# Attention and two expert layers on one core: filler matmuls in batch 0, 12 transposes a unit, and a later place for w_out's scale

## The chip, the cores and the metric
The kernel runs on one core of one Trainium2 chip. The metric is the device time of one execution in microseconds. The core's engines are TensorE (PE), VectorE (DVE), ScalarE (ACT), GpSimd (POOL) and SyncE (SP, which here issues the DMAs); each works through a queue of its own in order, and waits on semaphores where it needs another engine's result.

## What is computed
The reference in short; the three parts are chained.

```python
# q, k, v: (4 batches, 8 heads, 576, 64)
out_d  = softmax(q_d k_d^T / 8) v_d          # q_d, k_d, v_d: means over 4 neighbours, 144 rows
local  = softmax(where(|i - j| < 4, q k^T / 8, -1e9)) v
x      = (repeat(out_d, 4) + local)           # -> 2304 tokens x 512

xn     = x / sqrt(mean(x * x) + 1e-6) * rms_g
g      = xn @ w_gate                          # 512 x 1536
x      = (g * sigmoid(g) * (xn @ w_val)) @ w_out   # 1536 x 512

h      = relu(x @ w_in)                       # 512 x 2048
out    = (s * h * h + b) @ w_out2             # 2048 x 512
```

## The kernel before
**Precision.** The products of the two expert layers run in 16-bit floats: each operand is split into a high and a low part, and three of the four partial products are summed, so one product of 128 x 288 over 512 takes 12 matmuls (`pg` for the gate, `pvl` for the value, L708). The weights come as 8-byte numbers; `fetch` (L614) loads a chunk and turns it into f32 on ACT (L624, L625) and DVE (L626, L630), and `halves` (L125) scales it and splits it into the two parts, either on ACT and DVE (L127, L128) or on POOL and ACT (L130 to L132).

**Stages.** Attention of batch 0 comes first, in four units of two heads (`early_unit`). A unit loads q, k and v, turns q and k by PE (`tp`, copied by ACT at L428), forms the local scores `sl` and the downsampled scores `sd`, two softmaxes, turns the probabilities (`tpl`, `tpd`), and multiplies with v (`pvd`, `pl`). When four units are through, `norm` sums the squares (`ssn`, L570), takes the root on POOL (r, then three bf16 parts rp, L575 to L581), spreads it by PE (`rb`, L586) and writes the scaled tokens into X (L595). Then the blocks of 288 tokens follow. Blocks 0 and 1 go together (`main01`): 24 pairs of gate and value products, for the four parts of the weights in turn (three pairs for each part and block), and then the out product (`po`, L729) of both blocks, 144 matmuls each. Attention of batch 1 is emitted in small steps between them.

**Weights.** The generator `rest` (L804) emits the preparation of the four weight parts (`prep_gv`: 8 chunks of 384 KB, the maximum by PE as `st`, then the splits), and then of w_out (`weigh`: 12 chunks of 512 KB, each squared by ACT into accw; `abo` casts the sums on POOL, `so` adds them on PE at L671, DVE makes the scale sgo, and 12 splits follow). The steps of `rest` are pulled one by one from the loops that emit attention and pairs; two at every step of `main01`.

**What sets the order.** The program is written as a list of tiles and instructions; when it is built, a scheduler puts each engine's instructions into one fixed order, by the order in which the code emits them, by priorities, and by its estimate of when inputs are ready. `queued(name)` (L312) holds back all that is emitted in it until two instructions noted in `gates[name]` are issued. Part 0 of the weights is under no gate; part 1 is under gates[1], the second softmax of batch 0's last unit; parts 2 and 3 and w_out are under gates[2], the first half of the norm (L597). On the chip nothing changes places any more: an instruction that waits holds all that is behind it on its engine.

**Buffers.** PSUM tiles named tp, tpl and tpd of batch 0, st, so, pg, pvl and po share one pool of four; sl has two, pl and pvd one together, sd, ssn and rb one together. The SBUF tile u, which a pair needs from ACT's tanh to POOL's low part, has three. Chunks whose 8-byte form does not fit in place are staged in a ring of four and two more (`staging`, L606).

Of the kernel before, what the change touches and what calls it, by code (L numbers as in the profile page):

```python
# [20 lines left out]
NP = H // 2  # L21
# [20 lines left out]
EARLY = 2  # L42
CAP0 = 100
# [26 lines left out]
def kernel(  # L70
# [49 lines left out]
    ENG = [(dve, pool)] * NPART + [dve]  # L120
# [110 lines left out]
    def load_unit(b, hp, qkf, vd, vw):  # L231
        h0 = 2 * hp
        for t, src in enumerate((q, k)):
            for h in range(2):
                if b == 0:
                    sp.dma_start(out=qkf[:, t, h], in_=src[b, h0 + h].rearrange("(p c) d -> p c d", c=6))
                else:
                    sp.dma_start(out=qkf[:, t, :, h, :], in_=src[b, h0 + h].rearrange("(c p) d -> p c d", p=GR))
# [105 lines left out]
    def values_d(vdh, PdT, scale, pairs=LL):  # L344
        pvd = pV.tile([128, SD], F32, tag="v", name="pvd")
        n_ = 2 * len(pairs) - 1
# [13 lines left out]
    def values_l(b, hp, js, vh, PlT, od, scale, pairs=LL):  # L360
        pl = pV.tile([128, 320], F32, tag="v", name="pl")
        for j in js:
# [26 lines left out]

    def turned(b, n, name):  # L390
        if b == 0:
            return mmp.tile([128, 3, n], F32, tag="mm", name=name)
        return pS.tile([128, 3, n], F32, tag="s", name=name)

    def early_unit(b, hp, sq_sum):
# [18 lines left out]
        for t in range(2):  # L414
            qT = qkT[:, S * t:S * t + S]
            qT = qT.rearrange("p (a c) -> p c a", c=6) if b == 0 else qT.rearrange("p (c a) -> p c a", c=6)
# [20 lines left out]
        def local(js):  # L437
            sl = pS.tile([128, 5, WIN], F32, tag="s", name="sl")
            for p0 in (0, 64):
# [18 lines left out]
        sd = pX.tile([128, 3, SD], F32, tag="x", name="sd")  # L458
        for o, q0 in ((0, 0), (1, 64), (2, SD - 64)):
# [22 lines left out]
        if b == 0 and hp == NP - 1:  # L482
            gates[1] = tuple(last)
        yield
        od = values_d(vs.unsqueeze(1), PdT, 0.25, ((0, 0),))
# [562 lines left out]
```

## Time and profile before
| what | value |
|---|---|
| median of 3 runs | 1107.35 us (1106.99 to 1108.79) |
| the profiled execution's own time | 1106.15 us |
| its span, first to last instruction | 1104.4 us |
| PE busy | 1003.6 us (91%) |
| DVE busy | 592.8 us (54%) |
| ACT busy | 521.4 us (47%) |
| POOL busy | 339.5 us (31%) |
| mean granted TensorE clock | 0.926 |

The times of runs hold what lies around the span, 1.75 us in the profiled execution. Busy time is an average over the whole run; the stages differ, so the windows of the trace are read stage by stage. The granted clock is the share of full speed (2.4 GHz) that TensorE was given; 0.50 is 1.2 GHz. Names are those of the program; W is the tile W1, which holds the weights' chunks and, early on, other things of the same place. Block 2's first matmul starts at 301.6 us, and blocks 2 to 7 and the second expert layer make up the rest.

### The profile page before, as it was taken

The numbers are of one execution on the slowest core, as the hardware profiler recorded it, in microseconds if no ns is written. First come the engines' busy times: TensorE is split into PE (matmuls) and PEld (weight loads), VectorE is DVE, ScalarE is ACT, GpSimd is POOL, SyncE is SP. The second block draws the span as 40 slices with busy tenths as digits, with TensorE's granted clock in tenths as the row PEclk, the third lists the DMA queues.
The fourth block names the chain that finished last, engine by engine and source line by source line (L and its number), as shares of the span: only waits on it lengthen the run. The fifth ranks groups of instructions, "written<-read, shape, count | busy, mean of one in ns | idle before, by whom it ended". The sixth has DMA issues, their size and how long they took to land.

```text
span 1104.4 us, 20466 instructions
## 1 busy us (share of the span) xinstructions
PE 1003.6 (91%) x8204; PEld 685.4 (62%) x8206; DVE 592.8 (54%) x1255; ACT 521.4 (47%) x1174; POOL 339.5 (31%) x433
## 2 busy tenths in 40 slices
PE   5775686899988989898999999999999999999998
PEld 4663564678866767676778667755554545455553
DVE  3766996642187764576762876656341414234241
ACT  3655778643255554355644777756140413223140
POOL 6435674246144545453644213621000000000000
PEclk7675885899988989998999999999999999999999
DMA  8733456100035542145511442400000000000000
GB/s 195 212 87 98 137 156 174 36 20 13 1 67 91 116 88 49 39 84 90 117 38 39 134 134 77 160 32 1 29 1 29 1 20 11 10 20 1 29 1 29
DMA packets 120431, 73.59 MB, mean 67 GB/s; under 512 B 102161, under 2 KB 108305, under 8 KB 120337
## 3 DMA queue, kind: packets, MB, share of 16 engines
q1 hardware_dynamic: 120336, 72.29, 26.1%
q8 instruction: 64, 1.05, 0.4%
q14 instruction: 31, 0.25, 0.1%
HBM read 54.97 MB, written 4.72 MB: 54 GB/s over the span
## 4 chain that ended last, share of the span: by engine, by line
PE 66%; DMA 13%; DVE 10%; ACT 6%; issue 3%; POOL 2%; SPq 1%; DVEq 0%; POOLq 0%; ACTq 0%
PE y L1010 17%; PE ph L990 16%; PE po L729 8%; PE pvl L708 8%; PE pg L708 8%; DMA stg<-in_moe_w_in_dram 3%; DMA qkT<-qk 3%; DMA stg<-in_moe_w_out_dram 2%; DVE W L630 2%; DVE stg L626 2%; DMA vd<-in_v_dram 2%; ACT stg L625 1%; PE pl L367 1%; PE pvd L352 1%; ACT W L624 1%
## 5 line engine op out<-in xcount | busy, mean ns | idle before, releaser
L708 PEld LDWEIGHTS <-W 128*128 128x128 f16 x2304 | 229.1, 101 | 88.9 <-issue 23.9
L990 PE MATMUL ph<-X,W 128*128 128x384 f16 x1152 | 196.6, 326 | 0.4 <-DVE s4o L673 0.3
L708 PE MATMUL pg<-X,W 128*128 128x288 f16 x1152 | 170.2, 296 | 15.0 <-DVE u L715 11.0
L708 PE MATMUL pvl<-X,W 128*128 128x288 f16 x1152 | 172.3, 295 | 0.6 <-DVE m L647 0.5
L990 PEld LDWEIGHTS <-W 128*128 128x128 f16 x1152 | 112.6, 98 | 81.5 <-issue 1.2
L1010 PE MATMUL y<-W 128*128 128x512 f16 x648 | 151.6, 379 | 0.0
L729 PEld LDWEIGHTS <-W 128*128 128x128 f16 x1152 | 111.5, 98 | 31.1 <-issue 2.8
L729 PE MATMUL po<-g,W 128*128 128x288 f16 x1008 | 129.0, 287 | 1.6 <-DVE u L715 0.9
L994 ACT ACTIVATE r<-ph 128x384 f32<-128x384 f32 x96 | 47.0, 490 | 175.8 <-PE ph L990 126.1
L719 POOL TENSOR_TENSOR g<-u,g 128x288 f16<-128x288 f32 x84 | 72.1, 859 | 140.3 <-ACT g L718 106.1
L1010 PEld LDWEIGHTS <-W 128*128 128x128 f16 x648 | 63.4, 98 | 70.9
L190 DVE SCALAR_TENSOR_TENSOR r<-ph,r 128x384 f32<-128x384 f32 x96 | 53.5, 557 | 59.5 <-ACT r L994 59.5
L1015 DVE SCALAR_TENSOR_TENSOR ys<-y,ccol,bcol 128x512 f32<-128x512 f32 x18 | 13.5, 751 | 121.1 <-PE y L1010 118.9
L718 ACT ACTIVATE g<-u 128x288 f16<-128x288 f32 x84 | 36.8, 438 | 77.7 <-DVE u L190 72.6
L715 DVE SCALAR_TENSOR_TENSOR u<-u,pvl 128x288 f32<-128x288 f32 x96 | 42.7, 447 | 45.7 <-PE pvl L708 42.2
L626 DVE SCALAR_TENSOR_TENSOR stg<-stg 128x512 int32<-128x512 int32 (+1 forms) x56 | 42.3, 756 | 35.0 <-ACT stg L625 34.4
L998 DVE TENSOR_TENSOR W<-r,W 128x384 f16<-128x384 f32 x72 | 40.1, 557 | 36.6 <-ACT W L997 36.6
L997 ACT ACTIVATE W<-r 128x384 f16<-128x384 f32 x72 | 37.5, 521 | 39.9 <-DVE r L190 39.9
L714 ACT ACTIVATE u<-pg,tsc 128x288 f32<-128x288 f32 x96 | 47.1, 492 | 16.5 <-PE pg L708 15.7
L1010 PE MATMUL y<-W,r2b 128*128 128x512 f16 x216 | 50.0, 379 | 0.0
L630 DVE SCALAR_TENSOR_TENSOR W<-W,stg 128x512 int32<-128x512 int32 (+1 forms) x56 | 47.9, 857 | 2.9 <-ACT W L624 2.3
L624 ACT ACTIVATE W<-stg 128x512 f32<-128x512 f32 (+1 forms) x56 | 36.0, 645 | 21.0 <-DMA stg<-in_moe_w_out_dram 10.0
(260 smaller groups left out, 1462.1 us busy)
## 6 DMA issues: line engine op xcount, KB each, us to landing
stg<-in_moe_w_out_dram SPq DMA_DIRECT2D x28, 512.0 KB
stg<-in_moe_w_in_dram SPq DMA_DIRECT2D x16, 512.0 KB
W<-in_moe_w_gate_dram SPq DMA_DIRECT2D x12, 384.0 KB
out_dram<-ys SPq DMA_DIRECT2D x18, 256.0 KB
qkf<-in_q_dram SPq DMA_DIRECT2D x26, 144.0 KB
qkf<-in_k_dram SPq DMA_DIRECT2D x26, 144.0 KB
vd<-in_v_dram SPq DMA_DIRECT2D x13, 288.0 KB
W<-in_moe_w_val_dram SPq DMA_DIRECT2D x8, 384.0 KB
```

The source lines that it names most:

```text
L190: (eng or dve).scalar_tensor_tensor(out=o, in0=a, scalar=s, in1=b, op0=ALU.mult, op1=ALU.mult)
L624: act.activation(out=dst, in_=stg[:, :, 1].bitcast(F32), func=AF.Copy, scale=2.0 ** -112)
L626: ins = dve.scalar_tensor_tensor(out=stg[:, :, 0], in0=stg[:, :, 1], scalar=-2 ** 31, in1=stg[:, :, 0], op0=ALU.bitwise_and, op1=ALU.bitwi ...
L630: dve.scalar_tensor_tensor(out=di, in0=di, scalar=3, in1=stg[:, :, 0], op0=ALU.logical_shift_left, op1=ALU.bitwise_or)
L708: pe.matmul(out=acc, lhsT=Cgv.half(o, FP, lw)[:, f0 * 128:f0 * 128 + 128], rhs=X16[:, kc, 3 * blk:3 * blk + 3, lx, :], start=i == 0, stop= ...
L714: act.activation(out=u, in_=ps[0], func=AF.Tanh, scale=tsc[:, part:part + 1])
L715: dve.scalar_tensor_tensor(out=u, in0=u, scalar=1.0, in1=ps[1], op0=ALU.add, op1=ALU.mult)
L719: pool.tensor_tensor(out=lo, in0=u, in1=hi, op=ALU.subtract)
L729: pe.matmul(out=acc, lhsT=Co.half(fc * 512, 512, lw)[:, m * 128:(m + 1) * 128], rhs=g16(fc)[:, lx, :], start=i == 0, stop=i == 35)
L990: pe.matmul(out=acc, lhsT=C2.half((p * KC + kc) * 512, 512, lw)[:, f0 * 128:f0 * 128 + 128], rhs=X16[:, kc, 4 * blk:4 * blk + 4, lx, :], s ...
L994: act.activation(out=r, in_=acc, func=AF.Relu, scale=2.0 ** -23)
L1010: pe.matmul(out=y, lhsT=src[:, lx, tt * 128:(tt + 1) * 128], rhs=C3.half(fc * 512, 512, lw), start=i == 0, stop=i == 47)
```

## The change
Five edits. A helper `warm` writes matmuls of no use (ones_b against columns of the mask) into PSUM tiles of batch 0 right after they are allocated: 2 for each tp, tpl, sl and pl and for sd, 4 for pvd, 136 in all, each as wide as its tile. The loads of q and k of batch 0 take the form of batch 1, so that a row of 64 numbers (256 B) is a packet where six rows were one (1536 B), and both heads are turned by one transpose, 12 a unit. The value weights of parts 0 and 1 are split on ACT and DVE, no longer on POOL. The gates become three: part 1 behind the second unit's second softmax, part 2 behind the last unit's, part 3 and w_out behind the norm. Finally, the steps of `rest` that the loop of blocks 0 and 1 may pull end after 12 x 4 + 12 steps, that is after w_out's chunks; w_out's scale, `so` and the splits are emitted when all 24 pairs are.

```diff
+WARMB = 1
+WARM = (2, 2, 2, 4, 2)
...
-    ENG = [(dve, pool)] * NPART + [dve]
+    ENG = [(dve, dve), (dve, dve), (dve, pool), (dve, pool), dve]
...
-                if b == 0:
-                    sp.dma_start(out=qkf[:, t, h], in_=src[b, h0 + h].rearrange("(p c) d -> p c d", c=6))
-                else:
-                    sp.dma_start(out=qkf[:, t, :, h, :], in_=src[b, h0 + h].rearrange("(c p) d -> p c d", p=GR))
+                sp.dma_start(out=qkf[:, t, :, h, :], in_=src[b, h0 + h].rearrange("(c p) d -> p c d", p=GR))
...
+    def warm(b, t, n):
+
+        if b < WARMB:
+            for _ in range(n):
+                pe.matmul(out=t, lhsT=ones_b, rhs=warm_in[:, :t.shape[1]], start=True, stop=True, skip_group_check=True)
+
     def turned(b, n, name):
         if b == 0:
-            return mmp.tile([128, 3, n], F32, tag="mm", name=name)
+            t = mmp.tile([128, 3, n], F32, tag="mm", name=name)
+            warm(b, t.rearrange("p a b -> p (a b)"), WARM[0])
+            return t
...
-                    c = 3 * g + i
-                    if b == 0:
-                        for h in range(2):
-                            pe.matmul(out=tp[64 * h:64 * h + 64, i, :], lhsT=qkf[:, t, h, c, :],
-                                      rhs=ident_f[:GR, :GR], start=True, stop=True, skip_group_check=True)
-                    else:
-                        pe.transpose(out=tp[:, i, :], in_=qkf[:, t, c].rearrange("p h d -> p (h d)"),
-                                     identity=ident_f[:GR, :GR])
+                    pe.transpose(out=tp[:, i, :], in_=qkf[:, t, 3 * g + i].rearrange("p h d -> p (h d)"),
+                                 identity=ident_f[:GR, :GR])
...
-        if b == 0 and hp == NP - 1:
-            gates[1] = tuple(last)
+        if b == 0 and hp % 2:
+            gates[1 + hp // 2] = tuple(last)
...
         if b == 0 and hh == 0:
-            gates[2] = tuple(last)
+            gates[3] = tuple(last)
...
-                with queued(min(p_, 2)) if p_ else nullcontext():
+                with queued(min(p_, 3)) if p_ else nullcontext():
...
+    steps = [0]
...
+            steps[0] += 1
             yield
...
                     for _ in range(REST):
-                        next(rest_it, None)
+                        if steps[0] < 12 * NPART + NF1:
+                            next(rest_it, None)
```

The first place is PE's queue around `so`, before. The ninth pair's pvl and other attention stand ahead of these rows; qk_1444 holds turned probabilities of a unit of batch 1, W_86 is W1.

```order
L444 MATMUL sl<-qkT_1720 64x70 x10
L367 MATMUL pl<-q_b,qk_1444 64x64 x5
L461 MATMUL sd<-X 64x144 x5
L367 MATMUL pl<-q_b,qk_1444 64x64
L461 MATMUL sd<-X 64x144
L367 MATMUL pl<-q_b,qk_1444 64x64 x2
L671 LDWEIGHTS ones_b
L671 MATMUL so<-abo,ones_b 128x12
L708 LDWEIGHTS W_86
L708 MATMUL pg<-X,W_86 128x288
```
Behind `so` the tenth pair begins.

The same queue after: here pg and pvl are those of the 24th pair.

```order
L716 LDWEIGHTS W_86
L716 MATMUL pg<-X,W_86 128x288
L716 LDWEIGHTS W_86
L716 MATMUL pvl<-X,W_86 128x288
L679 LDWEIGHTS ones_b
L679 MATMUL so<-abo,ones_b 128x12
L716 LDWEIGHTS W_86
L716 MATMUL pvl<-X,W_86 128x288
```
`so` now stands within the last pair, ahead of the last eleven matmuls of its pvl. The end of that pvl and what follows it, a little later in the same queue:

```order
L716 MATMUL pvl<-X,W_86 128x288
L461 MATMUL tpl<-ident_f,ch 70x128 x5
L447 LDWEIGHTS ident_b
L447 MATMUL sl<-mask,ident_b 64x280
L447 LDWEIGHTS ident_b
L447 MATMUL sl<-mask,ident_b 64x280
L451 MATMUL sl<-P_l 64x70 x8
L486 MATMUL tpd<-ident_f,de_2338 72x128 x3
L737 LDWEIGHTS W_86
L737 MATMUL po<-g_1259,W_86 128x288
```
Attention of batch 1 (turned probabilities, a group of sl, a group of tpd) stands between the last pair and the first po; the four accumulators of po's block 0 follow.

The second place is POOL's queue at the first half of the norm, before (r and rp are the norm's root and its bf16 parts; L130 and L132 are multiplies and subtractions of weight splits).

```order
L575 TENSOR_TENSOR r<-ms,mhalf 96x3
L132 TENSOR_TENSOR W_86<-W_86 128x384
L577 TENSOR_SCALAR r<-r 96x3
L579 CAST rp_906<-r 96x3
L581 TENSOR_TENSOR r<-r,rp_906 96x3
L130 TENSOR_TENSOR W_86<-W_86,rs 128x384 x3
L132 TENSOR_TENSOR W_86<-W_86 128x384
L579 CAST rp_907<-r 96x3
L130 TENSOR_TENSOR W_86<-W_86,rs 128x384
L581 TENSOR_TENSOR r<-r,rp_907 96x3
L132 TENSOR_TENSOR W_86<-W_86 128x384
L579 CAST rp_908<-r 96x3
```
And after:

```order
L388 TENSOR_TENSOR sqsum<-sqsum,sq 128x288 x4
L583 TENSOR_TENSOR r<-ms,mhalf 96x3
L585 TENSOR_SCALAR r<-r 96x3
L587 CAST rp_994<-r 96x3
L589 TENSOR_TENSOR r<-r,rp_994 96x3
L587 CAST rp_995<-r 96x3
L589 TENSOR_TENSOR r<-r,rp_995 96x3
L587 CAST rp_996<-r 96x3
```
The weight splits between r and the third rp (rp_906 to rp_908 before, rp_994 to rp_996 after) are gone from this queue; they are on ACT and DVE.

The third place is ACT's queue in front of the norm's first copies X<-xn, before (L624, L625 conversions of a chunk, L127, L131 first halves of splits, L385 squares):

```order
L624 ACTIVATE W_86<-W_86 128x384
L625 ACTIVATE W_86<-W_86 128x384
L131 ACTIVATE W_86<-W_86 128x384
L385 ACTIVATE sq<-X 128x288
L131 ACTIVATE W_86<-W_86 128x384 x3
L127 ACTIVATE W_86<-W_86,rs 128x384 x2
L595 ACTIVATE X<-xn 128x3x96 x2
L127 ACTIVATE W_86<-W_86,rs 128x384
```
And after, where L632 and L633 are the conversions, L129 the first halves, L387 the squares and L603 the copies:

```order
L632 ACTIVATE W_86<-stg 128x384
L633 ACTIVATE stg<-stg 128x384
L387 ACTIVATE sq<-X 128x288
L129 ACTIVATE W_86<-W_86,rs 128x384
L632 ACTIVATE W_86<-stg 128x384
L633 ACTIVATE stg<-stg 128x384
L387 ACTIVATE sq<-X 128x288
L129 ACTIVATE W_86<-W_86,rs 128x384 x4
L603 ACTIVATE X<-xn 128x3x96 x2
L129 ACTIVATE W_86<-W_86,rs 128x384
```
Three parts of the weights (24 chunks) have their conversions ahead of the first copy after, two (16 chunks) before. On all engines the rows from block 2 on are the same before and after.

## Rows read from the trace of the kernel before
**Rows 1.** The busy shares by slices: PE and its granted clock, 40 slices of 27.6 us.
```profile
PE   5775686899988989898999999999999999999998
...
PEclk7675885899988989998999999999999999999999
```

**Rows 2.** Windows: us, then PE, PEld, DVE, ACT, POOL busy, PEclk, DMA share, GB/s.
```profile
60.00:92.00 32.00, 21.13 (x247) 17.62 (x244) 22.36 (x50) 18.52 (x50) 12.90 (x14) 0.67 0.40 108
92.00:104.60 12.60, 3.35 (x24) 2.56 (x25) 5.39 (x17) 3.83 (x9) 9.53 (x16) 0.50 0.22 57
104.60:157.00 52.40, 43.28 (x379) 32.35 (x378) 48.86 (x107) 38.37 (x93) 29.39 (x34) 0.90 0.41 125
157.00:197.10 40.10, 24.51 (x190) 17.83 (x191) 28.47 (x47) 30.14 (x78) 19.72 (x21) 0.53 0.62 170
197.10:264.20 67.10, 67.06 (x602) 50.63 (x602) 34.24 (x82) 35.42 (x84) 28.90 (x38) 0.95 0.08 21
264.20:301.60 37.40, 37.40 (x321) 30.13 (x319) 7.30 (x20) 10.69 (x29) 8.42 (x16) 1.00 0.01 3
```

**Rows 3.** Timeline of PE: start, us, what, [idle before <-releaser].
```profile
154.97 1.63 PE L708 MATMUL pvl<-X,W 128*128 128x288 f16 x12
...
174.56 0.85 PE L478 MATMUL tpd<-ident_f,de 128*72 128x128 f32 x3
...
197.14 0.17 PE L671 MATMUL so<-abo,ones_b 128*128 128x12 bf16 x1 [3.41 <-POOL abo L669]
...
286.21 14.99 PE L729 MATMUL po<-X,W 128*128 128x288 f16 x121
```

**Rows 4.** Timeline of SyncE: the DMA issues of w_out.
```profile
141.80 11.16 SPq L621 DMA_DIRECT2D stg<-in_moe_w_out_dram  x4
```

**Rows 5.** Timeline of PE at the end of batch 0, before block 0.
```profile
75.30 0.80 PE L367 MATMUL pl<-gx 70*64 70x64 f32 x20
...
91.83 1.12 PE L570 MATMUL ssn<-ones_f,sqsum 128*96 128x1 f32 x6 [0.42 <-POOL sqsum L386]
...
104.60 0.40 PE L708 MATMUL pg<-X,W 128*128 128x288 f16 x1 [1.41 <-ACT X L595]
```

**Rows 6.** Timeline of DVE: first and last of the twelve w_out splits.
```profile
200.94 0.75 DVE L128 SCALAR_TENSOR_TENSOR W<-W,sgo 128x512 f16<-128x512 f32 x1 [0.35 <-ACT W L127]
...
222.88 0.75 DVE L128 SCALAR_TENSOR_TENSOR W<-W,sgo 128x512 f16<-128x512 f32 x1
```

**Rows 7.** Timeline of ACT: weight conversions; a copy without a stride.
```profile
68.82 0.98 ACT L624 ACTIVATE W<-W 128x384 f32<-128x384 f32 x2
...
75.74 0.43 ACT L428 ACTIVATE qkT<-tp 128x288 f32<-128x288 f32 x1
```

**Rows 8.** Timeline of POOL: multiplies in the norm; the cast ahead of so.
```profile
97.07 2.39 POOL L130 TENSOR_TENSOR W<-W,rs 128x384 f32<-128x384 f32 x3 [0.18 <-DVE invg L190]
...
196.89 0.20 POOL L669 CAST abo<-accw 128x12 bf16<-128x12 f32 x1 [4.49 <-ACT wsq L666]
```

**Rows 9.** Instructions by line and shape, 0 to 300 us: busy, mean ns | idle before.
```profile
L423 PE MATMUL tp<-ident_f,W 96*64 96x96 f32 x144 | 12.7, 345 | 2.2 <-DMA W<-in_q_dram 1.9 <-POOL mask L177 0.3
...
L426 PE MATMUL tp<-ident_f,qkf 96*128 96x96 f32 x48 | 10.9, 313 | 0.3 <-ACT qkT L428 0.3
...
L128 DVE SCALAR_TENSOR_TENSOR W<-W,rs 128x384 f16<-128x384 f32 x16 | 10.8, 678 | 6.4 <-ACT W L127 6.4
...
L428 ACT ACTIVATE gx<-tp 128x288 f32<-128x288 f32 x4 | 2.7, 682 | 0.0
```

**Rows 10.** DMA queue at 16:32, 52:62 and 140:157 us: packets, MB, share.
```profile
q1 hardware_dynamic: 5097, 3.52, 101.0%
...
q1 hardware_dynamic: 3984, 1.21, 52.3%
...
q1 hardware_dynamic: 1446, 2.54, 48.7%
```

**Rows 11.** The chain of waits up to 130 us: one load of a weight chunk.
```profile
82.29 8.52 DMA W<-in_moe_w_val_dram
```

More of the change, by code (lines that the diff above doesn't have):

```diff
@@ L342, with values_d @@
     LL = ((0, 0), (0, 1), (1, 0))
-    def values_d(vdh, PdT, scale, pairs=LL):
+    def values_d(vdh, PdT, scale, pairs=LL, warm_b=None):
         pvd = pV.tile([128, SD], F32, tag="v", name="pvd")
+        if warm_b is not None:
+            warm(warm_b, pvd, WARM[3])
         n_ = 2 * len(pairs) - 1
@@ L361, in values_l @@
         pl = pV.tile([128, 320], F32, tag="v", name="pl")
+        warm(b, pl, WARM[4])
         for j in js:
@@ L388 @@
     JS = (range(5), range(5, 9))
+    warm_in = mask.rearrange("p j k -> p (j k)")
+    def warm(b, t, n):
+        if b < WARMB:
+            for _ in range(n):
+                pe.matmul(out=t, lhsT=ones_b, rhs=warm_in[:, :t.shape[1]], start=True, stop=True, skip_group_check=True)
     def turned(b, n, name):
         if b == 0:
-            return mmp.tile([128, 3, n], F32, tag="mm", name=name)
+            t = mmp.tile([128, 3, n], F32, tag="mm", name=name)
+            warm(b, t.rearrange("p a b -> p (a b)"), WARM[0])
+            return t
         return pS.tile([128, 3, n], F32, tag="s", name=name)
@@ L415, in early_unit @@
             qT = qkT[:, S * t:S * t + S]
-            qT = qT.rearrange("p (a c) -> p c a", c=6) if b == 0 else qT.rearrange("p (c a) -> p c a", c=6)
+            qT = qT.rearrange("p (c a) -> p c a", c=6)
             for g in range(2):
@@ L438, in local @@
             sl = pS.tile([128, 5, WIN], F32, tag="s", name="sl")
+            warm(b, sl.rearrange("p a b -> p (a b)"), WARM[1])
             for p0 in (0, 64):
@@ L458, in early_unit @@
         sd = pX.tile([128, 3, SD], F32, tag="x", name="sd")
+        warm(b, sd.rearrange("p a b -> p (a b)"), WARM[2])
         for o, q0 in ((0, 0), (1, 64), (2, SD - 64)):
@@ L481, in early_unit @@
         a = softmax_l(sl, JS[1], 1.0 / 8, 1.0, 1, dve if b == 0 and hp == NP - 1 else pool, a)
-        if b == 0 and hp == NP - 1:
-            gates[1] = tuple(last)
+        if b == 0 and hp % 2:
+            gates[1 + hp // 2] = tuple(last)
         yield
-        od = values_d(vs.unsqueeze(1), PdT, 0.25, ((0, 0),))
+        od = values_d(vs.unsqueeze(1), PdT, 0.25, ((0, 0),), b)
         turn(a, JS[1])
@@ L827 @@
         if hp < NP - 1:
-            st_ = (W1[:GR, o:o + 1536].rearrange("p (t h c d) -> p t h c d", t=2, c=6, h=2),
+            st_ = (W1[:GR, o:o + 1536].rearrange("p (t c h d) -> p t c h d", t=2, c=6, h=2),
                    W1[:72, o + 1536:o + 2560].rearrange("p (a r d) -> p a r d", a=4, r=4))
         else:
-            st_ = (ap.tile([GR, 2, 2, 6, D], F32, tag="qkf", name="qkf"),
+            st_ = (ap.tile([GR, 2, 6, 2, D], F32, tag="qkf", name="qkf"),
                    ap.tile([72, 4, 4, D], F32, tag="vd", name="vd"))
```

## The prediction
> **What bounds the kernel now.** I read the busy shares by slices first. TensorE (PE) is busy eight tenths or more of each slice from the eighth on; it has holes in the first seven slices (27.6 us each), and there the granted clock falls too [rows 1]. So a gain has to come out of the first 200 us. The windows then cut the stretch up to the first matmul of block 2 at 301.6 us [rows 2]. From block 2 on each engine's queue holds the same instructions in the same order before and after, so I let the rest of the run keep its length and forecast only when block 2 starts. This stretch has two stages.
>
> Stage A, 0 to 104.6 us: attention of batch 0, then its norm, then the first gate matmul (pg) [rows 5]. Stage B, 104.6 to 301.6 us: the 24 gate/value pairs and the out product of blocks 0 and 1, with attention of batch 1 strewn in. PE's work in stage B, busy time by granted clock, is 43.28 x 0.90 + 24.51 x 0.53 + 67.06 x 0.95 + 37.40 = 153.1 us; the stage lasts 197.0 us, so 43.9 us are lost: 13.4, 27.1, 3.4 and 0 in its four windows. The 27.1 us have one place. The value product (pvl) of the ninth pair starts at 154.97 us; behind it PE's queue has only attention and then `so`, one matmul of 0.17 us that starts at 197.14 us after 3.41 us of waiting for POOL's `abo` [rows 3]. PE takes its queue in order: `so` stands in front of the tenth pair, `abo` needs the squares of all twelve w_out chunks, and these chunks are loaded only from 141.8 us on [rows 4], behind the weights of part 3. Whatever parts 1 and 2 were ready for, PE could not reach it.
>
> **The `so` moved behind the pairs.** After the change `so` stands inside the last pair. The removed loss is 27.1 us, if the fifteen pairs find their weights. Part 3 is needed only after 18 pairs, 18 x 24 x 0.124 = 54 us of PE's work (14.99 us for 121 matmuls of 288 columns [rows 3]). What comes late instead is the chain behind `so`. Before, it ran from 197.14 us to the end of the twelfth w_out split on VectorE (DVE) at 222.88 + 0.75 = 223.6 us, 26.5 us [rows 3, 6], under the remaining pairs. Now only this covers it: half a pair (1.4 us), some attention (eight transposes at 0.85 / 3 us [rows 3] and ten small matmuls of sl, between 3 and 4 us), and block 0's out product (po), 144 x 0.124 = 17.9 us, whose last 12 matmuls (1.5 us) need the last split. The new wait is 26.5 + 1.5 - 23.3 = 4.7 us. If DVE's own 12 x 0.75 = 9 us set the pace nothing is left to wait for; behind a crowded DVE it may be 12 us. I take 4.7, as 26.5 is that chain's own row. The conversions, splits and attention of the hole now compete with the pairs for DVE and ScalarE (ACT); in stage B they are busy 118.9 and 114.6 us [rows 2] against PE's 153, so I take 3 us (0 to 10) for meeting. Stage B becomes 197.0 - 27.1 + 4.7 + 3 = **177.6 us**.
>
> **The gates of the weight parts.** Part 1's conversions now go behind the second unit's softmax, part 2's behind the last unit's, so chunks that had landed need no longer stand until 68.8 us [rows 7]. Between the pl at 75.30 us and the norm's ssn at 91.83 us lie 16.5 us [rows 5]; the attention in it is some 7.5 us of PE's work, 9 us are waits on the ACT and DVE chains of weights. Half of that is taken, as part 2's conversions now come into the same stretch: -4.5 us (from -9 to 0).
>
> **Value weights of parts 0 and 1 on ACT and DVE.** Three of POOL's multiplies, 2.39 us, stood between the norm's steps [rows 8], six such pieces in all, at 0.80 us 4.8 us; from ssn to the first pg are 12.8 us [rows 5]. After the change nothing stands between r and the last rp on POOL, but DVE gets 8 more splits of 0.68 us [rows 9], of which some lie in front of the norm's multiplies: -4 us (from -4.8 to 0).
>
> **The transposes.** The 24 matmuls of a unit leave 48 records of 12.7 / 144 us, 4.2 us; the 12 transposes of a unit of batch 1 are busy for 10.9 / 4 = 2.7 us [rows 9]: 1.5 us less of PE in each of four units. The ACT copy of 288 columns takes 0.68 us with a stride [rows 9] and 0.43 without [rows 7], 16 times 0.25 us less. Nearly all of both lies under the loads; I take -1 us (from -4 to 0).
>
> **The loads.** q and k of batch 0 (16 x 144 KB, 2.36 MB) now come in packets of 256 B instead of 1536 B. The early stretch is bound by the queue (its share is 101% at 16 to 32 us [rows 10]). What a small packet costs: at 52 to 62 us, when batch 1's q and k of that form come in, the queue moves 1.21 MB in 52.3% of 10 us, 231 GB/s of queue time; with w_out's large ones at 140 to 157 us it is 2.54 MB in 48.7% of 17 us, 307 GB/s [rows 10]. So 2.36 MB take 10.2 against 7.7 us: +2.5 us at most from these rows, and nothing by the row of 16 to 32 us (3.52 MB in 101% of 16 us, 218 GB/s, with large packets among them). I take +1.5.
> The Trainium skill, "DMA: Bandwidth & Descriptors", Specifications, speaks against this edit: it wants at least 512 B a transfer, since below that the DMA engine reads, modifies and writes. The 231 GB/s show no doubling; were it so here, the time is that of rival four.
>
> **The matmuls of no use.** 136 with 44,128 columns in all: 44,128 / 288 x 0.124 = 19.0 us at 2.4 GHz, 38 us at 1.2 GHz. They stand right behind the allocation of a PSUM tile and ahead of its real matmuls, so they fall into a wait where the inputs are later than the buffer. From 60 to 104.6 us PE idles 44.6 - 24.5 = 20.1 us and its clock is 0.67 and 0.50 [rows 2]. If the clock rises to 0.9 there, 24.5 us of work become about 17 us, but on the path stand waits for other engines, not PE's work. What is hidden and what is not I set against each other: 0, between -6 and +19 (nothing hidden).
>
> Stage A: -4.5 - 4 - 1 + 1.5 + 0 = -8, first pg at **96.6 us** (88 to 110).
>
> **Sum.** -8 - 19.4 = -27.4 us. The profiled execution has 1106.15 us, of which 1104.4 are span; it lies 1.2 us under the median of the runs. 1106.15 - 27.4 = 1078.7; beside the median some 1079.9. I say **1079 us**.
>
> **Rivals.**
> First, the hole closes only by half: a new wait in the strict order holds PE. The candidate is on POOL: `abo` there stands ahead of the low parts (g) of the fourteenth pair and later; if w_out's squares are as late as now (`abo` at 196.89 us after 4.49 us of waiting for them [rows 8]), u's three buffers run out, and ACT's tanh and PE stand three pairs later. For it: the loads from 141.8 us on wait for staging buffers. Against: PE has by then about 80 us of its work done and the wait is short. It gives back half of 27.1: **1092**. 15 in 100.
> Second, the matmuls of no use lie on the path: their 19 us are added, and the higher clock gives back 4: **1094**. For it: in a run of work without waits on inputs they have nothing to hide in. 8 in 100.
> Third, slower: part 2's eight chunks are converted on ACT ahead of the norm's copies (24 chunks before them, 16 until now), and ACT waits in order. One chunk took 8.52 us to land [rows 11]; two at a time, eight are 8 x 4.26 = 34 us. Then the first pg comes at 138.6 us, stage B has its weights early and is 170 us long: 308.6, that is **1113**. It decides from a first pg at 301.6 - 177.6 = 124 us on. Against it: the DMA engines have long pauses between 60 and 92 us (share 0.40 [rows 2]), so the chunks can come early. 5 in 100.
> Fourth, small packets take twice the queue's time: 2.36 MB at 218 GB/s are 10.8 us more, nearly all before the first units: **1089**. 4 in 100.
> Fifth, more gain: the 13.4 us lost before 157 us close too, as parts 1 and 2 are ready earlier, and the norm takes all of its 9 us: **1057**. 10 in 100.
>
> **How the numbers follow.** My case has 58 in 100 and by the ends of its terms 1062 to 1095. The range 1058 to 1098 also takes in rivals one, two and four and part of the fifth, and leaves out the slower one and the tails. A difference under 0.2% (2.2 us) can't be told from none: faster 0.92, same 0.02, slower 0.06 (rival three and a piece of one and two at once).
>
> **What would show it.** Right: `so` waits little or not at all, pg and pvl run through from the first to the 24th pair, and stage B is near 178 us; the first pg comes between 88 and 110 us; po's first matmuls wait a few us for w_out splits by DVE; on POOL the norm's steps from r to the third rp follow within 3 us. ACT's waits before the norm name DMA if rival three holds. Wrong: pairs after the fourteenth that wait for DVE or ACT behind `abo` (rival one); a PE busy with matmuls of ones_b while nothing is waited for, and a first pg after 110 us (two); q and k loads that land later than before (four). If the first pg comes early and block 2 does not, the loss lies in stage B.

## The result, and the profile after

The changed kernel takes 1068.9 us (median of 4 runs, 1066.9 to 1074.3) where the kernel before takes 1107.6: a ratio of 0.966 (0.963 to 0.970). Its profiled execution is the longest of these four, 1074.31 us with a span of 1072.4; against the profiled execution of before that is 31.8 us less, the medians lie 38.8 us apart. The sum of the prediction was 27.4 us.

The slices of the changed kernel, 26.8 us each, PE's busy tenths and its granted clock:

```profile
PE   7985999999889899888999999999999999999998
...
PEclk9986989999989899989999999999999999999999
```
PE is busy eight tenths or more from the second slice on, but for the fourth (26.8 us from 80.4 us on, where the norm stands), and the hole of [rows 1] in the sixth and seventh slices is gone. The windows, with the columns of [rows 2]; the first gate matmul is at 88.8 us and block 2 starts at 269 us:

```profile
0.00:45.00 45.00, 37.69 (x408) 26.50 (x408) 25.24 (x57) 25.28 (x71) 28.16 (x53) 1.00 0.96 219
45.00:60.00 15.00, 13.93 (x171) 9.38 (x170) 14.86 (x35) 11.07 (x34) 5.64 (x7) 1.00 0.98 271
60.00:88.80 28.80, 18.13 (x218) 14.54 (x216) 24.77 (x60) 17.35 (x42) 11.89 (x16) 0.70 0.66 193
88.80:104.60 15.80, 10.58 (x71) 7.41 (x71) 12.14 (x28) 11.24 (x25) 7.52 (x9) 0.72 0.12 29
104.60:157.00 52.40, 49.63 (x415) 36.42 (x414) 45.30 (x95) 40.24 (x100) 27.67 (x30) 0.93 0.39 129
157.00:197.10 40.10, 40.10 (x378) 30.89 (x377) 24.93 (x55) 25.21 (x67) 18.39 (x24) 0.96 0.30 87
197.10:226.70 29.60, 27.64 (x246) 19.69 (x241) 11.09 (x35) 11.65 (x32) 9.42 (x12) 0.94 0.09 21
226.70:269.00 42.30, 41.54 (x392) 33.01 (x393) 18.51 (x38) 22.40 (x50) 20.80 (x31) 1.00 0.04 9
```
From 157 to 197.1 us, where PE had 24.51 us of work at half the clock [rows 2], it now has 40.10 of 40.10. The clock is at full speed through the first 60 us, and DVE, not PE, fills the stretch ahead of the first gate matmul (24.77 of 28.8 us). The landmarks on PE, in answer to [rows 3, 5]:

```profile
35.40 0.80 PE L369 MATMUL pl<-PlT,vh 70*64 70x64 f32 x20
...
79.19 1.12 PE L578 MATMUL ssn<-ones_f,sqsum 128*96 128x1 f32 x6 [0.17 <-POOL sqsum L388]
...
88.76 0.40 PE L716 MATMUL pg<-X,W 128*128 128x288 f16 x1 [1.09 <-ACT X L603]
...
221.19 0.17 PE L679 MATMUL so<-abo,ones_b 128*128 128x12 bf16 x1
...
226.68 1.64 PE L737 MATMUL po<-g,W 128*128 128x288 f16 x12 [0.30 <-ACT W L129]
...
269.09 1.63 PE L716 MATMUL pg<-X,W 128*128 128x288 f16 x12
```
Stage A is 15.8 us shorter (104.6 to 88.8 us), stage B 16.5 us (196.8 to 180.3 us, taken from timeline row to timeline row); behind block 2's start both kernels take 803 us. `so` waits for nothing. The last row but one is the first po: it waited 0.30 us.

### The profile page after: what moved, and what is told of

Same layout as the page of the kernel before. It is cut to its first block, busy times and chain, and to the rows that moved or that the text cites. A ratio compares the mean times of both kernels' runs of the same rounds, so it can differ in the third digit from the quotient of the medians.

```text
span 1072.4 us, 20420 instructions
## 1 busy us (share of the span) xinstructions
PE 1002.0 (93%) x8196; PEld 677.8 (63%) x8198; DVE 593.5 (55%) x1263; ACT 519.8 (48%) x1174; POOL 328.0 (31%) x417
## 4 chain that ended last, share of the span: by engine, by line
PE 73%; DVE 12%; DMA 7%; ACT 4%; issue 2%; POOL 1%; SPq 0%; POOLq 0%; DVEq 0%
PE y L1021 17%; PE ph L1001 17%; PE po L737 12%; PE pg L716 8%; PE pvl L716 8%; DMA qkT<-qk 3%; DMA stg<-in_moe_w_in_dram 2%; PE pl L369 2%; DVE W L638 2%; DVE stg L634 1%; DMA stg<-in_moe_w_out_dram 1%; PE pvd L353 1%; PE sl L302 1%; PE sd L287 1%; DMA PlT<-P_l 1%
## 5 line engine op out<-in xcount | busy, mean ns | idle before, releaser
L716 PEld LDWEIGHTS <-W 128*128 128x128 f16 x2304 | 228.7, 101 | 83.8 <-issue 19.5
L716 PE MATMUL pg<-X,W 128*128 128x288 f16 x1152 | 171.9, 298 | 14.3 <-DVE u L723 12.2
L716 PE MATMUL pvl<-X,W 128*128 128x288 f16 x1152 | 169.8, 292 | 0.0
L723 DVE SCALAR_TENSOR_TENSOR u<-u,pvl 128x288 f32<-128x288 f32 x96 | 42.5, 446 | 45.0 <-PE pvl L716 40.2
L634 DVE SCALAR_TENSOR_TENSOR stg<-stg 128x512 int32<-128x512 int32 (+1 forms) x56 | 40.1, 715 | 26.1 <-ACT stg L633 25.9
L638 DVE SCALAR_TENSOR_TENSOR W<-W,stg 128x512 int32<-128x512 int32 (+1 forms) x56 | 45.7, 817 | 2.8 <-ACT W L632 2.3
L632 ACT ACTIVATE W<-stg 128x512 f32<-128x512 f32 (+1 forms) x56 | 36.2, 648 | 19.3 <-DMA stg<-in_moe_w_in_dram 9.4
```

The costliest lines, as they stand in the source:

```text
L634: ins = dve.scalar_tensor_tensor(out=stg[:, :, 0], in0=stg[:, :, 1], scalar=-2 ** 31, in1=stg[:, :, 0], op0=ALU.bitwise_and, op1=ALU.bitwi ...
L638: dve.scalar_tensor_tensor(out=di, in0=di, scalar=3, in1=stg[:, :, 0], op0=ALU.logical_shift_left, op1=ALU.bitwise_or)
L716: pe.matmul(out=acc, lhsT=Cgv.half(o, FP, lw)[:, f0 * 128:f0 * 128 + 128], rhs=X16[:, kc, 3 * blk:3 * blk + 3, lx, :], start=i == 0, stop= ...
L723: dve.scalar_tensor_tensor(out=u, in0=u, scalar=1.0, in1=ps[1], op0=ALU.add, op1=ALU.mult)
```

## The experiments

All kernels in one table; times of stages are those of the profiled executions, ratios are to the kernel before, run on the same chip. The kernels were run in sets on several chips, on which the kernel before took 1104.0 to 1108.3 us, so kernels of different sets are compared by their ratios.

| kernel | median us | ratio | first pl | first pg | pg to block 2 | block 2 to end |
|---|---|---|---|---|---|---|
| before | 1107.6 | | 48.2 | 104.6 | 196.8 | 803.0 |
| the change | 1068.9 | 0.966 (0.963 to 0.970) | 35.4 | 88.8 | 180.3 | 803.3 |
| the change, again | 1071.6 | 0.966 (0.962 to 0.970) | 35.4 | 88.2 | 178.7 | 803.2 |
| A: before, `so` late | 1077.2 | 0.973 (0.968 to 0.977) | 47.0 | 103.7 | 177.5 | 794.6 |
| B: change, `so` early | 1080.1 | 0.976 (0.971 to 0.981) | 34.8 | 85.7 | 187.0 | 804.6 |
| C: before, fillers | 1103.3 | 0.999 (0.997 to 1.002) | 51.7 | 106.9 | 194.4 | 798.6 |
| D: change, no fillers | 1063.0 | 0.959 (0.955 to 0.963) | 31.3 | 95.6 | 168.5 | 799.5 |
| E: change, old loads and turning | 1074.7 | 0.974 (0.969 to 0.978) | 51.4 | 107.3 | 167.2 | 796.0 |
| F: change, old turning only | 1070.5 | 0.969 (0.967 to 0.971) | 44.2 | 98.5 | 169.6 | 801.0 |
| G: A, chunks loaded later | 1077.9 | 0.977 (0.973 to 0.980) | 46.8 | 105.1 | 176.0 | 795.2 |
| H: change, old gates | 1066.8 | 0.967 (0.962 to 0.972) | 35.5 | 83.3 | 174.1 | 802.2 |
| I: change, old splits | 1074.1 | 0.973 (0.968 to 0.977) | 36.2 | 96.8 | 170.3 | 803.9 |
| J: before, `so` late, new loads and turning | 1074.6 | 0.972 (0.969 to 0.975) | 30.6 | 95.6 | 172.8 | 803.0 |
| K: change, no fillers, old gates | 1069.8 | 0.968 (0.964 to 0.972) | 31.5 | 89.2 | 175.0 | 808.1 |

First pl is the first product of probabilities and v, the first unit's; each edit makes the scheduler lay out every engine's queue anew, so the rows of the table do not add up.

**The change once more.** No edit.

> The changed kernel once more. Its profiled execution took 1074.3 us, its other runs 1066.9 to 1069. If the 5.4 us lie ahead of block 2, a second profile whose own time is near 1068 shows the first gate matmul or block 2's start (88.8 and 269.1 us in the first profile) earlier by about 5 us; if they lie behind, block 2 starts at 269 us again and the tail is 798 us instead of 803. Time 1066 to 1070 us by both.

Its profiled execution has 1071.9 us: block 2 starts 2.2 us earlier, at 266.93 us, and the rest is 803.2 us again. So a part of the spread of the runs lies ahead of block 2; where the shorter runs of 1067 us save the rest was not seen in a profile.

**`so` moved, alone, and everything but that (A, B).** A is the kernel before with only the cap on the steps; B is the changed kernel without it.

```diff
 for _ in range(REST):
-    if steps[0] < 12 * NPART + NF1:
-        next(rest_it, None)
+    next(rest_it, None)
```

> The kernel before with one edit, w_out's scale behind all 24 pairs. By the prediction's step this alone takes 27.1 us of hole and gives 7.7 us back: 197.0 us from the first gate matmul to block 2 become 178, time 1086 to 1091 us, first gate matmul at 104 to 105 us as before. Rival: without the new gates the later weight parts come late, and half of the hole stays as waits of the pairs: time 1095 us or more.

> The changed kernel with w_out's scale emitted as early as before (no end to the steps that the loop of blocks 0 and 1 pulls). Theory 1: the hole behind the ninth pair comes back, 17 to 27 us: time 1085 to 1096 us, with so waiting for POOL's abo and no gate or value matmul for some 20 us ahead of it. Rival: since the weights are loaded and converted some 15 us earlier now, so finds abo sooner and the hole is less than 8 us: time below 1077 us.

A on PE: first pg, `so`, and the start of block 2.

```profile
103.72 0.40 PE L708 MATMUL pg<-X,W 128*128 128x288 f16 x1 [1.41 <-ACT X L595]
...
232.63 0.18 PE L671 MATMUL so<-abo,ones_b 128*128 128x12 bf16 x1
...
281.17 1.63 PE L708 MATMUL pg<-X,W 128*128 128x288 f16 x12
```
281.2 - 103.7 = 177.5 us, where the prediction had worked out 177.6, and the first gate matmul has moved by 0.9 us only. The expectation's time of 1086 to 1091 was still 9 us too long, since behind block 2 this kernel takes 794.6 instead of 803.0 us: its queues differ there too, in the first blocks after it.

B on PE, and then the windows of gate and value matmuls alone (L716) around it (us, PE, PEld, clock, DMA share, GB/s):

```profile
149.39 1.28 PE L461 MATMUL tpl<-ident_f,ch 128*70 128x128 f32 x5 [6.09 <-POOL ch L332]
...
159.89 0.19 PE L679 MATMUL so<-abo,ones_b 128*128 128x12 bf16 x1
159.94 3.04 PE L716 MATMUL pg<-X,W 128*128 128x288 f16 x12
```
```profile
125.00:145.00 20.00, 5.80 (x31) 3.71 (x31) 0.83 0.54 159
145.00:165.00 20.00, 4.79 (x19) 2.71 (x19) 0.50 0.48 155
```
The hole is back, smaller and in another place: no gate or value matmul from 135.5 to 159.9 us, 24.5 us against 40.6 before, `so` at 159.9 instead of 197.1 us, and without a wait of its own, as attention stands ahead of it. In B w_out is loaded from 103.7 us on, before only from 141.8 [rows 4]. So `so` standing early costs 8.5 us here (1080.1 against 1071.6 in the same set of runs), not 17 to 27, and the other edits had closed the greater part of the hole from the other side. Theory 1 had the length of the stretch and missed its price; the rival had the mechanism (`abo` comes sooner), and the price was a little above its 8 us. Both missed the time.

**The fillers alone, and everything but them (C, D).** C is the kernel before with `warm` and its calls, D the changed kernel with

```diff
-WARMB = 1
+WARMB = 0
```

> The kernel before with one edit, the 136 matmuls of no use. Theory 1 (the fillers lift the clock and little else; they gave some 7 us ahead of the first gate matmul in the changed kernel, where it came at 95.6 us without and at 88.8 us with them): first gate matmul at 97 to 101 us instead of 104.6, hole behind the ninth pair as before, time 1099 to 1104 us. Rival (the units of batch 0 wait for loads, POOL and ACT here, not for PE): no change within 2 us, or later by up to 5.

> The changed kernel without its matmuls of no use; all else as in it. Theory 1: the gain ahead of the first gate matmul (15.8 us) comes from the order of the queues (POOL no longer holds the turned q and k behind the sums of v that wait for a load) and from the new gates; the fillers are worth 0 to 4 us: first gate matmul at 89 to 93 us, time 1067 to 1073 us. Theory 2: it comes from the clock that the fillers hold at 1.00 in the first 60 us (0.72 and 0.82 before): without them the first gate matmul is back at 100 to 104 us and the time 1080 to 1085 us. The granted clock of the first 45 us falls to about 0.7 by both.

C in windows of 30 us (columns as in [rows 2]):

```profile
0.00:30.00 30.00, 17.17 (x172) 10.52 (x173) 6.68 (x14) 6.71 (x12) 15.26 (x39) 1.00 0.90 182
30.00:60.00 30.00, 28.50 (x331) 19.07 (x331) 21.90 (x48) 21.78 (x59) 13.67 (x15) 0.89 0.65 188
```
The clock stands at 1.00 and 0.89 with the old loads and the old order, and the first gate matmul comes at 106.9 us, 2.3 us later than without; the time is that of before (0.999, 0.997 to 1.002). In D the clock is 0.84 in the first 45 us (0.7 was expected) and 0.56 from 30 to 60 us, and yet the first pl comes 4 us earlier than in the changed kernel; only from there to the first gate matmul it loses, 64.4 us against 53.4. It then has block 2 at 264.1 us, earlier than with fillers (266.9 and 269.1), and is the shortest kernel of all: its 4 runs (1060.9 to 1065.4) lie below all of the changed kernel's in the same set (1067.9 to 1072.6). The first gate matmul at 95.6 us lies between the two theories, the time below both: that the clock makes the gain (1080 us and more without it) is out.

**The loads and the turning (E, F).** E takes back the form of the loads and the 24 matmuls, F only the 24 matmuls:

```diff
-pe.transpose(out=tp[:, i, :], in_=qkf[:, t, 3 * g + i].rearrange("p h d -> p (h d)"),
-             identity=ident_f[:GR, :GR])
+c = 3 * g + i
+if b == 0:
+    for h in range(2):
+        pe.matmul(out=tp[64 * h:64 * h + 64, i, :], lhsT=qkf[:, t, c, h, :],
+                  rhs=ident_f[:GR, :GR], start=True, stop=True, skip_group_check=True)
+else:
+    pe.transpose(out=tp[:, i, :], in_=qkf[:, t, c].rearrange("p h d -> p (h d)"),
+                 identity=ident_f[:GR, :GR])
```

> The changed kernel with the loads and the turning of batch 0's q and k as before (1536 B packets, 24 matmuls a unit, copies with a stride). The first unit's first pl came at 48 us before and in the kernel with w_out's scale late alone (47 us), at 35 us after and at 31 us without the fillers. Theory 1: it is this part that does it, by the shorter copies and transposes and the order that follows from them: first pl at 43 to 48 us, first gate matmul 3 to 10 us later than 88.8. Rival (gates and splits do it): first pl at 35 us, first gate matmul within 2 us of 88.8 or earlier by the 2.5 us that large packets would save.

> The changed kernel with the 24 matmuls of 64 x 96 a unit for turning q and k, but the loads of the change (256 B packets) and so the copies without a stride. With the old loads and turning together the first gate matmul came at 107.3 us instead of 88.8, and ACT waited 14.3 us for weight chunks in the first 60 us instead of 1.3. Theory 1 (order: ACT's queue puts conversions of chunks that have not landed ahead of the copies of turned q and k; here they stand ahead of some of them again): ACT's waits for weights 5 to 14 us, first gate matmul at 97 to 107 us. Rival (it is the form of the load and of the copies, not the transposes): first gate matmul at 88 to 92 us.

E puts the first gate matmul back to 107.3 us, F to 98.5 us: of the 18.5 us between the changed kernel and E, more than theory 1 had said, about half hangs on the transposes, the rest on the form of the loads and copies. F meets its theory 1 (ACT's conversions): ACT waits 10.0 us for weights. Where the delay arises can be read off the queues of ACT and POOL: ACT copies the turned q and k of a unit (gx for the third), POOL sums them, and behind these stand in PE's queue the third unit's sl or sd and then the first pl. The last of ACT's gx copies, before, after (its last two in one row) and in E:

```profile
41.87 0.69 ACT L428 ACTIVATE gx<-tp 128x288 f32<-128x288 f32 x1
```
```profile
31.25 0.71 ACT L434 ACTIVATE gx<-tp 128x288 f32<-128x288 f32 x2
```
```profile
46.03 0.71 ACT L443 ACTIVATE gx<-tp 128x288 f32<-128x288 f32 x1
```
They ended at 42.6, 32.0 and 46.7 us. Ahead of them ACT's queue has the conversions of eight weight chunks before and in E (8.7 and 8.8 us of work, 10.6 and 13.6 us of waiting for chunks to land), of three after (3.3 us of work, 1.3 us of waiting). On POOL, before (columns as in [rows 8]), the sum of gx stands behind a sum of v that waited 6.74 us for its load, and that v is batch 1's:

```profile
42.26 1.44 POOL L249 TENSOR_TENSOR vd<-vd 72x512 f32<-72x512 f32 x1 [6.74 <-DMA vd<-in_v_dram]
43.67 1.53 POOL L431 TENSOR_TENSOR gx<-gx 128x576 f32<-128x576 f32 x1
...
45.84 0.66 POOL L432 TENSOR_TENSOR X<-gx 128x288 f32<-128x288 f32 x1
```
The chain of waits of the kernel before goes through this load to PE:

```profile
34.21 7.92 DMA vd<-in_v_dram
...
46.55 1.71 PE sd L461 x12
48.26 1.26 PE pl L367 x20
```
But without it the sum would have come only 1.1 us earlier, as ACT's last copy had ended at 42.56. After, the gx sum stands ahead of it and follows ACT's copy at once:

```profile
32.03 1.52 POOL L437 TENSOR_TENSOR gx<-gx 128x576 f32<-128x576 f32 x1 [2.33 <-ACT gx L434]
33.52 1.26 POOL L248 TENSOR_TENSOR vd<-vd 72x512 f32<-72x512 f32 x1
34.74 0.66 POOL L438 TENSOR_TENSOR X<-gx 128x288 f32<-128x288 f32 x1
...
42.12 1.28 POOL L248 TENSOR_TENSOR vd<-vd 72x512 f32<-72x512 f32 x1 [2.70 <-DMA vd<-in_v_dram]
```
In E the sum stands behind that v again, and yet what it waited for last was ACT's copy:

```profile
46.81 1.20 POOL L446 TENSOR_TENSOR gx<-gx 128x576 f32<-128x576 f32 x1 [0.22 <-ACT gx L443]
```
In the built order the count is plain. In all six kernels that turn with 24 matmuls (before, A, C, E, F, G) eight conversions stand ahead of ACT's last gx copy, which ends at 41.2 to 46.7 us, and five sums of v ahead of the gx sum, which starts 0.1 (E, G) to 3.3 us (F) behind the copy; the first pl comes at 44.2 to 51.7. In the seven with 12 transposes three conversions and three sums of v stand ahead, the copy ends at 29.9 to 32.8 us, the sum starts 0.1 us behind it, and the first pl comes at 30.6 to 36.2. So of the 16.0 us between the change and E at the first pl 14.8 lie ahead of the end of ACT's last copy, and POOL's place for v adds 3.3 us at most. The total of waits does not sort the kernels: POOL's for loads of v in the first 60 us are 12.3 us in F and 15.6 in K, whose first pl comes 13 us earlier. In C and E PE's last matmuls for gx, too, start only past 44 us (30.3 in the change); what held them was not followed. That one of these orders alone does it was not tried; both go with the first pl in all thirteen.

**ACT's waits for weight chunks (G).** ACT, too, waited for loads in the first 60 us: 10.6 us before, 1.3 us after, 14.3 in E, where more conversions of chunks stand ahead of the copies of turned q and k. G is A with three of these chunks loaded behind all units:

```diff
-LOADW = (0, 1, 1, 1)
+LOADW = (0, 0, 0, 0)
```

> The kernel before with w_out's scale late, and with one more edit: the three weight chunks whose loads were emitted between the units' loads come after all of them, so that no conversion of a chunk stands ahead of the first units' copies on ACT. Old loads, old turning, no fillers. Theory 1 (these waits, 9.2 us on ACT and 17.8 us on POOL for v, hold the first units): the waits for weights in the first 60 us fall below 4 us, the first pl comes at 36 to 42 us instead of 47, first gate matmul up to 6 us earlier than 103.7; time 1070 to 1077 us. Rival (the units are held by their own loads or by DVE): first pl at 45 to 48 us, first gate matmul no earlier or, since part 0 is converted later, up to 8 us later.

The waits of ACT in G, 0 to 60 us (total, times, longest):

```profile
ACT W L624 <- DMA W<-in_moe_w_gate_dram: 4.0, 1, 4.0
...
ACT W L624 <- DMA W<-in_moe_w_val_dram: 0.4, 1, 0.4
```
They fell from 9.2 to 4.4 us, and the first pl came at 46.8 instead of 47.0 us, the first gate matmul 1.4 us later: theory 1's times did not come. But the edit moved the loads and not the conversions. Eight of them still stand ahead of ACT's last gx copy, which ended at 42.4 us (41.3 in A), and POOL's gx sum, at 42.5 us in both kernels, waited for this copy in G, its fifth sum of v being through at 39.5 us:

```profile
42.48 1.42 POOL L431 TENSOR_TENSOR gx<-gx 128x576 f32<-128x576 f32 x1 [3.01 <-ACT gx L428]
```
So G takes POOL's wait for v off the path and gains nothing by it; that the conversions' place on ACT holds the units is left standing, and not tried alone.

**The gates and the splits (H, I).** H puts parts 1 and later under the two gates of before, I gives the value weights of parts 0 and 1 back to POOL, by this edit:

```diff
-    ENG = [(dve, dve), (dve, dve), (dve, pool), (dve, pool), dve]
+    ENG = [(dve, pool)] * NPART + [dve]
```

> The changed kernel with the two gates of before (part 1 behind the last unit's softmax, all later ones behind the first half of the norm). Theory 1: the gates set what ACT and DVE have to do between the first unit and the norm; with fewer conversions ahead of it the norm comes no later (first gate matmul 82 to 90 us), but parts 1 and 2 come late in the pairs: stage from the first gate matmul to block 2 5 to 15 us longer than 179; time 1073 to 1085 us. Rival (the prediction's step: the new gates shorten the way to the norm by 4.5 us): first gate matmul at 93 us, the later stage unchanged, time 1075 us.

> The changed kernel with the value weights of parts 0 and 1 split by POOL again. By the prediction's step POOL's splits come back between the norm's root and its third part: from ssn to the first gate matmul 12 to 13 us instead of 9.6, first gate matmul at 91 to 93 us, time 1073 to 1075 us. Rival: DVE, which is busy 24.8 of the 28.8 us ahead of the first gate matmul, is relieved of 8 splits (5.4 us) and the norm starts earlier by as much: first gate matmul at 86 to 88 us.

H is no slower than the change (0.967 against 0.966), and its first gate matmul comes 5 us earlier, its block 2 at 257.4 us; what the expectation feared for the pairs did not happen. (Its profiled execution, 1061.3 us, is the shortest of its four, 5.6 us under their median.) I has its first gate matmul at 96.8 us, 8 us later. POOL in I around ssn, which stood at 83.79 us after 4.67 us of waiting for the squares:

```profile
78.49 4.11 POOL L132 TENSOR_TENSOR W<-W,rs 128x384 f32<-128x384 f32 x4 [6.38 <-DVE m L657]
82.57 2.24 POOL L388 TENSOR_TENSOR sqsum<-sqsum,sq 128x288 f32<-128x288 f32 x2
85.24 3.98 POOL L132 TENSOR_TENSOR W<-W,rs 128x384 f32<-128x384 f32 x4 [0.43 <-DVE rs L660]
89.18 1.20 POOL L583 TENSOR_TENSOR r<-ms,mhalf 96x3 f32<-96x3 f32 x1
```
Four multiplies of a split stand ahead of the squares, four more ahead of the root. From ssn to the first gate matmul are 13.0 us here and 9.6 in the change: the 3.4 us of the prediction's kind; the other 4.6 lie ahead of ssn. The rival (a relieved DVE brings the norm forward) is out. At block 2 nothing is left of the 8 us: I starts it at 267.1 us.

**Two edits, three edits (J, K).** J is the kernel before with `so` late and with the new loads and transposes. K is the changed kernel without fillers and with the old gates.

> The kernel before with two of the five edits: w_out's scale late, and the loads and transposes of batch 1's form for batch 0. No fillers, old gates, POOL's splits as before. Theory 1: these two carry the whole gain: first pl at 31 to 36 us, first gate matmul at 88 to 97 us, 168 to 176 us from there to block 2, time 1060 to 1070 us. Rival (splits and gates are needed too, 8 us as when the splits alone were undone): 1074 us or more.

> The changed kernel without its fillers and without its new gates, that is three of the five edits. Without the fillers it took 1063.0 us, with the old gates 1066.8 us. If both savings add up: 1055 to 1061 us, first gate matmul at 86 to 92 us, block 2 at 254 to 260 us. If they are the same saving (DVE and ACT have less to do ahead of the norm): 1062 to 1068 us.

J starts block 2 at 268.4 us, where the changed kernel has 266.9 and 269.1: in the profiled executions two edits of five bring all of the gain up to there. Its median, 1074.6 us, lies where the rival put it, and by the ratios (0.972 against 0.966) it is some 7 us above the changed kernel; ahead of block 2 this difference was not seen. K starts block 2 at 264.2 us, as D does, so the savings of D and H do not add up. Its median of 1069.8 us is above both theories, and by its ratio K is no better than the change; its profiled execution, the longest of its four (1063.4 to 1074.2), takes 808.1 us behind block 2. D, at 0.959, remains the best.

## Why the prediction was right, and where it was not

**The `so` behind the pairs: right, in size too.** 27.1 us of hole out, 7.7 us back, 177.6 us: A has 177.5. In the whole change stage B came out at 180.3 (and 178.7) us. That they agree to 0.1 us is luck: A's windows, counted as the prediction counts, give 157.4 us of PE's work and 20.0 us lost, where 153.1 and 24.5 had been summed. The term of 4.7 us for po's wait was too large. In A po waited 0.55 us for a split's first half on ACT. In the change the chain from `so` to the end of the last split took 25.1 us, as worked out (26.5), by these rows of DVE,

```profile
226.66 0.75 DVE L130 SCALAR_TENSOR_TENSOR W<-W,sgo 128x512 f16<-128x512 f32 x1 [0.79 <-ACT W L129]
...
244.86 1.39 DVE L130 SCALAR_TENSOR_TENSOR W<-W,sgo 128x512 f16<-128x512 f32 x1 [0.79 <-ACT W L129]
```
but PE waited only 1.17 + 0.49 + 0.30 us in it, because some 6 us of batch 1's attention lay ahead of and between the matmuls of po, where 3 to 4 us were counted: 25.1 + 1.5 - (1.4 + 6 + 17.9) leaves 1.3 us. The other side of the balance was clock, below. That `so` was the cause is shown by A alone; that it is not the only way to close the hole is shown by B.

**The gates: wrong.** The stretch from the third unit's pl to ssn, of which the prediction took 4.5 us away, has 16.45 us after (62.74 to 79.19 us) and 16.5 before [rows 5]: nothing. H, whose first gate matmul comes 5 us earlier, shows that the new gates put work of weights ahead of the norm. What they do bring is an earlier load of the later weights: the queue's share from 60 to 75 us goes from the first to the second of these rows (before, then after: packets, MB, share),

```profile
q1 hardware_dynamic: 86, 0.08, 1.7%
```
```profile
q1 hardware_dynamic: 3477, 3.12, 74.7%
```
and w_out is issued from 109 us on (141.8 before, 120 in H). With `so` behind the pairs this is not needed (H); what it is worth with an early `so`, as in B, was not tried apart from the other edits.

**The splits off POOL: right at the first gate matmul, undersized.** 4 us predicted, 8 us measured there (I); the multiplies stood ahead of ssn as well, which the rows of the norm alone did not show. To block 2 this does not carry: I, F and J have their first gate matmul at 95.6 to 98.5 us and start block 2 at 267.1 to 268.4, where the change does (266.9 and 269.1). The prediction added what stage A gains to what stage B gains; here stage B gave it back.

**The transposes and the loads: the step that failed.** They were taken at -1 and +1.5 us, and E gives them 18.5 us at the first gate matmul. The prices were taken as busy time of PE and ACT and held to be hidden under the loads. What the edit really moved was the order of the queues: conversions of weight chunks ahead of ACT's copies of turned q and k, eight before and three after, and with them sums of v on POOL. The waits were in the trace: 10.6 us of ACT for chunks, and on the chain batch 1's v, 7.92 us, then POOL, sd, pl. The prediction compared the queues of PE, POOL and ACT around the norm and around `so`, and not around the first unit's pl. At block 2 these 18.5 us are worth 5 to 7 (274.5 against 267 to 269), as stage B gives most of them back: it is mostly the shorter, the later it begins (167 to 173 us with a first pg past 95 us in D, E, F, I and J, 180 with one at 88.8). That conversions and splits left over at its start then go with the pairs would be a reason, and is not shown; H, with 174.1 at 83.3, does not fit it.
The loads themselves did cost about what was taken. From 16 to 32 us the queue has

```profile
q1 hardware_dynamic: 8732, 3.36, 107.8%
```
that is 195 GB/s of queue time against 218 [rows 10], or 1.8 us more for 3.36 MB, an estimate, as other loads are among them. The doubling of rival four, 10.8 us of queue time in all, is not there. Every q and k packet now has 256 B, where the Trainium skill ("DMA: Bandwidth & Descriptors", Specifications) gives 512 B as the least for the full rate, with a read-modify-write below it.

**The fillers: net nothing, as predicted, but with two sides.** Alone they change nothing (C). In the change they bring the first gate matmul forward by 7 us (D 95.6, change 88.8) and leave the whole longer by 8.6 us (1071.6 against 1063.0 in one set of runs): about 3 to 5 us by block 2 and some 4 behind it, where D's queues also differ. They do lie on the path in part, as rival two had it: of the chain of waits up to the first pl (35.4 us) 9.7 us are fillers, and D, without them, has this pl 4.1 us earlier; the 19 us of the rival did not come. With the old gates they take nothing away: H has 0.967 with fillers, K 0.968 without.

**The rivals.** The new wait at `abo` did not come: `abo` ran at 170.08 us after 1.88 us of waiting, and the pairs behind it went on. The slower case (norm held by loads of part 2) did not come either; ACT waited 1.3 us for weights in the first 60 us. So the time came out 10 us below the likeliest case, half of it ahead of block 2 (269.1 us in the profile, where 274.2 was forecast), by the failed step, and inside the range because the range held stage A down to 88 us. That it is no further off is in part luck: 4.5 us for gates that gave nothing stood in for an edit that was priced at +0.5 and gave more.

**The size.** In the profiled executions stage A gave 15.8 us where 8 were forecast and stage B 16.5 where 19.4 were, 32.3 us for 27.4. The other runs of the change are some 5 us shorter than its profiled one; that part is not located.
Some sums of the prediction do not come out. Rival five takes off all 9 us of the norm, of which 4.5 were in the sum already; by its own terms it stands at 1061, not 1057. The ends of stage A's terms, added up, give a first gate matmul from 80.8 to 126 us, not 88 to 110, and with stage A at 110 the ends of stage B's terms give some 1107 us, not 1095.

## What to carry to other kernels

An instruction of 0.2 us that needs the last of a long row of loads belongs behind all work that does not need it; what it held up can be read as the stretch without any of that work, and what its own followers then wait for is the price.
Where a scheduler fixes the queues, the cost of an edit is not the busy time that it adds or removes: compare the queues of every engine at each landmark of the chain of waits, and look for work on data still being loaded (conversions of later weights on ACT, sums of the next batch's v on POOL) that has moved ahead of, or behind, something PE needs.
And build each part of a change alone and each part left out: here two of five edits carried most of the gain (J, 0.972 of 0.966), one took something away beside the other four, and the kernel without it is the best.
One profiled execution is one draw: stage times a few microseconds apart are no difference until the runs of both kernels lie apart.

## What the runs showed of the hardware that I had not expected

**A full clock that buys nothing.** In C PE was given 0.92 and 1.00 in the first 60 us instead of 0.72 and 0.82 (0 to 45 and 45 to 60 us), and no gain clear of noise came of it (0.999, 0.997 to 1.002): the units still wait there for loads, POOL and ACT, and 8.1 us of the chain up to C's first pl are the fillers themselves.

**Clock lost without idle time.** In the change PE is busy from 157 to 197 us without a gap, at a clock of 0.96. The gate matmuls behind a stretch of attention with narrow tiles ran at a granted clock of 0.50 (1.2 GHz, 177.4 to 180.1 us):

```profile
176.72 0.29 PE L353 MATMUL pvd<-P_d,vs 72*64 72x16 f32 x2
176.94 0.57 PE L716 MATMUL pvl<-X,W 128*128 128x288 f16 x2
177.31 3.09 PE L716 MATMUL pg<-X,W 128*128 128x288 f16 x12
```
3.09 us for 12, against 1.63 elsewhere [rows 3]. Such spells stand at 136 (behind 0.88 us of idling, too), 154, 178 and 208 us, each behind attention; in H there is none from 100 us to block 2. A busy share of 100% is thus not PE at its peak, and the order in which attention is strewn between the pairs may have a price of its own; no run varies that alone.

**Half speed behind one wait, full speed behind another.** Early in block 2, behind a wait for DVE, the change and D:

```profile
283.33 3.04 PE L716 MATMUL pg<-X,W 128*128 128x288 f16 x12 [3.86 <-DVE u L723]
```
```profile
297.34 1.63 PE L716 MATMUL pg<-X,W 128*128 128x288 f16 x12 [1.49 <-DVE u L723]
```
After 3.86 us of idling the 12 matmuls took 3.04 us, at a granted clock of 0.50; after 1.49 us they took 1.63, at 1.00. PE's work ahead of the two waits differs as well, so these are two cases and no rule.

**The rest of the run is not a constant.** The prediction let the 803 us behind block 2's start stand. With the same order there they were 803.0, 803.3, 803.2, 804.6 and 798.6 us (before, the change twice, B, C). E, F, H and K share another order, on all engines and in the DMA issues, and took 796.0, 801.0, 802.2 and 808.1 us: 12 us lie between executions of the same queues. So K's 808.1 us are not the price of its order, D's 799.5 no gain of its own that is shown, and what sets this part of the time from one execution to the next stays open.
